# Query and key transposes by transposing DMA for the third and later blocks of a fused attention and channel-mix kernel

One core of a Trainium2 chip. The metric is the device time of one execution in microseconds (us), lower is better. Times below are medians of several executions; "span" is the length of one profiled execution. A run is called slow here when it lies over 1.5% above the fastest of the same kernel in the same call, and fast otherwise. The granted clock is the share of its full speed that TensorE was given, as the profile records it.

## The reference

Retention attention (a state that decays by gamma at each token), followed by an RWKV channel mix. Cut to what matters; the kernel computes the recurrence in chunks of 128 tokens.

```python
# q, k, v: (4, 8, 768, 64) float32
for t in range(S):
    state = gamma * state + k[:, :, t] (outer) v[:, :, t]
    y[:, :, t] = q[:, :, t] @ state / sqrt(D)
x = y.transpose(0, 2, 1, 3).reshape(B, S, 512)
xk = mu_k * x + (1 - mu_k) * x_prev          # x_prev: x one token earlier
xr = mu_r * x + (1 - mu_r) * x_prev
kk = max(xk @ w_k, 0)                         # 512 -> 1024
out = sigmoid(xr @ w_r) * (kk * kk @ w_v)
```

There are 24 chunks of 128 tokens, two to a block, so 12 blocks (0 to 11).

## The kernel before

The order of all instructions is written by hand: `at(t, fn, ...)` puts a piece of work at a place `t`, all pieces are sorted by `t` and emitted, and each engine runs its own in that order. Twelve units are one block in the steady stage. Semaphores that make a reader wait for its writer follow from the tiles. `keys` and `squared` below are the channel mix's first product and its relu and square; "gate" is the product with `w_r`, "values" the one with `w_v`.

```python
ORDER = {"att": {"scale": (-11.82,), "first": (-6.14, 0.23),
                 "T": (-2.09, 2.5), "TC": (-0.47, 4.83),        # transposes, their copy
                 "S": (2.27, 4.47), "A": (3.18, 6.35), ...,     # state, scores
                 "dx": (11.71,), "xk": (18.04, 21.12), "xr": (21.16, 27.83)},
         "mix": {"G": (-1.27, -0.4, 3.31, 4.49), ...},
         "load": (1.19, 3.99),
         "start": {0: (-6.29, -4.12, -3.14, -2.71), ...}}       # places of blocks 0 to 3
# ... cut ...
def scale_k(n, c, eng):                  # POOL for blocks 2 to 11, DVE for 0 and 1
    ...
    eng.tensor_tensor(out=KS[n][:, e], in0=K32[n][:, e], in1=w, op=ALU.mult)

def transposes(c):                       # 16 on TensorE for one chunk
    PT[c] = psa.tile([P, 2, NJ, C], F16, name="pT", tag="a")
    needs(("ks", c))
    for i, src in enumerate((Q16, KS)):
        for h in range(H):
            r = slice(h % 2 * D, h % 2 * D + D)
            nc.tensor.transpose(PT[c][r, i, h // 2, :], heads(src, c, h, 1), ident)

def transposed(c):                       # ACT copies them from PSUM to SBUF
    QKT[c] = att.tile([P, 2, NJ, C], F16, name="qkT")
    nc.scalar.copy(out=QKT[c], in_=PT.pop(c))

def scores(c):                           # pA = ks . q, from qkT alone
    ... nc.tensor.matmul(PA[c][hp][:, j, :], lhsT=QKT[c][r, 1, j, :], rhs=QKT[c][r, 0, j, :], ...)

def differ(m, eng):                      # dx = x - x_prev, POOL from block 2 on
    ... eng.tensor_tensor(out=DX[m], in0=xcur, in1=xprev, op=ALU.subtract)
# ... cut ...
def attention(n, t0, w=1.0):
    start = n < 2
    if not start:
        at(o("scale"), scale_k, n, None, nc.gpsimd)
    if n + LDK < NBLK:                   # the key load of block n+2 right behind the scaling of n
        at((... if start else o("scale")) + 0.01, load_k, n + LDK)
    for i, c in enumerate((2 * n, 2 * n + 1)):
        at(o("T", i), transposes, c)
        at(o("TC", i), transposed, c)
        # ... state, scores, mask, result ...
# ... cut: first loads, all at one place, so in the order of these lines ...
for n in range(2):
    for c in range(2):
        at(t, load_q, n, c); at(t, load_k, n, c); at(t, load_v, n, c)
at(t, load_wk, 0); at(t, load_wk, 1)
at(t, load_q, 2); at(t, load_v, 2)
at(t, load_wr); at(t, load_wv, 0); at(t, load_wv, 1)
```

## Time and profile before

| | kernel before |
|---|---|
| time, median of 3 runs | 174.53 us (173.55 to 176.16) |
| span of the profiled run | 173.3 us, mean granted TensorE clock 0.961 |
| TensorE (PE) busy / idle in the span | 152.7 / 20.6 us |
| PE idle in the first 80 us | 16.5 us |
| hardware DMA queue of SP (keys, stores) | 11.64 MB, 27.0% of 16 engines |

DVE is VectorE, ACT ScalarE, POOL GpSimd, SP SyncE. An L number is a line of that kernel's own file, so the same work has other L numbers in another kernel. The first 80 us of PE alone; columns: stretch, length, PE busy (instructions), granted clock, DMA share (packet time over that of 16 engines; it goes above 1 here), GB/s:

```profile
20.00:40.00 20.00, 16.82 (x282) 0.83 1.37 178
40.00:60.00 20.00, 16.51 (x216) 0.83 1.11 124
60.00:80.00 20.00, 20.00 (x344) 1.00 1.26 158
```

PE has a few us of holes between 20 and 60 us and none after. The second view is the chain of waits in that ramp (start, length, what):

```profile
22.89 1.91 POOL ks L185
24.80 12.01 issue
36.85 1.90 POOL dx L286
38.74 1.86 POOL ks L185
...
43.23 6.52 DMA v<-in_v_dram
```

POOL scales the keys of block 2 at 22.89 us, waits for the difference of block 2 (36.85), scales block 3's keys right behind it and only then issues block 3's last loads. In the ramp the blocks thus hang on each other through POOL. The start of a block's difference `dx` is a good milestone for its progress, and I use it below.

### The profile page before, as it was taken

Reading aid. Unit: us, or ns where it says so; the run is one execution under the profiler, and the core shown is the slowest. Engines: PE = TensorE matmul, PEld = TensorE weight load, DVE = VectorE, ACT = ScalarE, POOL = GpSimd, SP = SyncE. Lnnn points to the kernel's source line nnn. Section 1 sums busy time; section 2 is a strip of 40 time slices with the busy share of each in tenths; the row PEclk is TensorE's granted clock in tenths of the full one; section 3 lists DMA queues with packets and bytes.
Section 4 is the critical chain, followed back from the end, with each engine's and each line's share of the span. In section 5 each row is a group of like instructions: output and inputs, shape, how many; then the busy total and the mean of one; then the engine's idle time right before and its main releaser. Section 6 shows DMA issues by size and latency. Waiting matters only on the chain.

```text
span 173.3 us, 5544 instructions
## 1 busy us (share of the span) xinstructions
PE 152.7 (88%) x2448; PEld 112.7 (65%) x2448; DVE 133.5 (77%) x232; ACT 92.0 (53%) x146; POOL 88.0 (51%) x81
## 2 busy tenths in 40 slices
PE   0477759999659999999999999999999999999990
PEld 0345549776436865977958759669588587595940
DVE  3469999958655995879989979898799797795312
ACT  3132207957220592881954927729739459275750
POOL 7999260049903996097974926909726040040000
PEclk9999957999956999999999999999999999999999
DMA  6999999995998399919999499697993003030303
GB/s 51 196 177 224 202 165 175 193 192 58 158 212 94 94 202 201 214 29 153 158 144 162 114 199 116 90 190 153 67 58 123 1 11 118 0 118 7 125 0 123
DMA packets 78504, 21.96 MB, mean 127 GB/s; under 512 B 72464, under 2 KB 75152, under 8 KB 78480
## 3 DMA queue, kind: packets, MB, share of 16 engines
q0 software_dynamic: 52880, 9.97, 68.0%
q1 hardware_dynamic: 24544, 11.64, 27.0%
q8 instruction: 19, 0.31, 0.7%
q10 hardware_dynamic: 1056, 0.00, 0.3%
q14 instruction: 5, 0.04, 0.1%
HBM read 24.22 MB, written 6.29 MB: 176 GB/s over the span
## 4 chain that ended last, share of the span: by engine, by line
PE 69%; POOL 11%; DMA 9%; issue 8%; DVE 0%; POOLq 0%; DVEq 0%
PE pV L157 23%; PE pZ L157 21%; PE pR L157 10%; DMA wk<-in_moe_w_k_dram 6%; PE pT L197 4%; DMA v<-in_v_dram 4%; PE pA L208 3%; POOL q L169 3%; PE pY L261 3%; POOL v L169 2%; POOL ks L185 2%; POOL k L169 2%; PE pY L157 2%; PE pS L235 2%; POOL dx L286 1%
## 5 line engine op out<-in xcount | busy, mean ns | idle before, releaser
L286 POOL TENSOR_TENSOR dx<-xT 128x1024 f32<-128x1024 f32 x10 | 18.9, 1890 | 62.0 <-DVE xT L272 62.0
L157 PE MATMUL pZ<-xk,wk 128*64 128x256 f16 x768 | 48.4, 278 | 2.0 <-DVE xk L294 2.0
L157 PE MATMUL pV<-wv,k 128*64 128x512 f16 x384 | 48.3, 389 | 0.0
L157 PEld LDWEIGHTS <-wk 128*64 128x64 f16 x768 | 42.2, 112 | 4.4 <-issue 2.6
L201 ACT COPY qkT<-pT 128x1024 f16<-128x1024 f16 x24 | 24.1, 1004 | 38.2 <-PE pT L197 38.2
L315 ACT ACTIVATE kr<-pZ 128x512 f32<-128x512 f32 x48 | 28.3, 590 | 25.3 <-PE pZ L157 25.3
L216 DVE TENSOR_TENSOR a2t<-pA,c_sb 128x512 f16<-128x512 f32 x48 | 30.6, 683 | 11.2 <-PE pA L208 11.1
L157 PEld LDWEIGHTS <-k 128*64 128x64 f16 x384 | 21.1, 112 | 15.3 <-issue 1.4
L316 ACT ACTIVATE k<-kr 128x512 f16<-128x512 f32 x48 | 30.2, 630 | 1.5
L294 DVE SCALAR_TENSOR_TENSOR xr<-dx,mur,xT 128x256 f16<-128x256 f32 x48 | 29.7, 662 | 0.0
L294 DVE SCALAR_TENSOR_TENSOR xk<-dx,muk,xT 128x256 f16<-128x256 f32 x48 | 26.4, 597 | 2.0 <-POOL dx L286 2.0
L346 DVE SCALAR_TENSOR_TENSOR osb<-pV,rsb 128x512 f32<-128x512 f32 x24 | 15.9, 686 | 11.5 <-ACT rsb L329 8.4
L157 PE MATMUL pR<-wr,xr 128*64 128x512 f16 x192 | 23.1, 379 | 0.0
L169 POOL DMA_DIRECT2D q<-in_q_dram x24 | 22.1, 930 | 0.8 <-POOLq L488 0.8
L169 POOL DMA_DIRECT2D v<-in_v_dram x24 | 21.6, 919 | 0.0
L185 POOL TENSOR_TENSOR ks<-k,csm_sb 128x1024 f16<-128x1024 f32 x10 | 19.5, 1946 | 0.1
L272 DVE TENSOR_TENSOR xT<-pY,gy_sb 128x512 f32<-128x512 f32 x24 | 16.3, 687 | 2.6 <-PE pY L261 2.2
L329 ACT ACTIVATE rsb<-pR 128x512 f32<-128x512 f32 x24 | 13.0, 594 | 8.9 <-PE pR L157 8.9
L157 PEld LDWEIGHTS <-xr 128*64 128x64 f16 x192 | 11.0, 110 | 8.7
L244 DVE TENSOR_TENSOR sbd<-pS,csm_sb 128x512 f16<-128x512 f32 x20 | 13.7, 686 | 3.4 <-PE pS L235 2.6
L197 PE MATMUL pT<-c_sb,q 128*64 128x128 f16 x192 | 10.3, 232 | 5.5 <-DMA q<-in_q_dram 5.5
L197 PE MATMUL pT<-c_sb,ks 128*64 128x128 f16 x192 | 10.3, 231 | 2.8 <-DVE ks L185 2.8
(29 smaller groups left out, 105.5 us busy)
## 6 DMA issues: line engine op xcount, KB each, us to landing
out_dram<-osb SPq DMA_DIRECT2D x24, 256.0 KB, 4.0
k<-in_k_dram SPq DMA_DIRECT2D x20, 256.0 KB, 6.7
q<-in_q_dram POOLq DMA_DIRECT2D x24, 128.0 KB, 6.0
v<-in_v_dram POOLq DMA_DIRECT2D x24, 128.0 KB, 7.0
k<-in_k_dram POOLq DMA_DIRECT2D x4, 256.0 KB, 4.7
wk<-in_moe_w_k_dram POOLq DMA_DIRECT2D x2, 512.0 KB, 11.0
wv<-in_moe_w_v_dram POOLq DMA_DIRECT2D x2, 512.0 KB, 20.7
wr<-in_moe_w_r_dram POOLq DMA_DIRECT2D x1, 512.0 KB, 18.5
```

The source lines that it names most:

```text
L157: nc.tensor.matmul(out[r], lhsT=lhsT[:, r], rhs=rhs, skip_group_check=True, **kw)
L169: eng.dma_start(out=tiles[n][:, i], in_=rows(x, n)[:, i])
L185: eng.tensor_tensor(out=KS[n][:, e], in0=K32[n][:, e], in1=w, op=ALU.mult)
L197: nc.tensor.transpose(PT[c][r, i, h // 2, :], heads(src, c, h, 1), ident)
L201: nc.scalar.copy(out=QKT[c], in_=PT.pop(c))
L216: nc.vector.tensor_tensor(out=A2[c][:, hp], in0=PA[c][hp], in1=causal[:, None, :].to_broadcast([P, NJ, C]), op=ALU.mult,)
L272: nc.vector.tensor_tensor(out=xT[b][:, :, col : col + C], in0=PY.pop(c), in1=gy[:, c % 2], op=ALU.mult)
L286: eng.tensor_tensor(out=DX[m], in0=xcur, in1=xprev, op=ALU.subtract)
L294: nc.vector.scalar_tensor_tensor(out=dst[m][:, j], in0=DX[m][:, j], scalar=mu[:, j : j + 1], in1=xprev[:, j], op0=ALU.mult, op1=ALU.add,)
L315: nc.scalar.activation(out=kr, in_=PZ.pop((m, g)), func=AF.Relu)
L316: nc.scalar.activation(out=K2[m][:, 2 * g : 2 * g + 2], in_=kr, func=AF.Square)
L346: nc.vector.scalar_tensor_tensor(out=osb, in0=PV.pop((m, tb)), scalar=1.0 / (KSC * KSC), in1=RS.pop((m, tb)), op0=ALU.mult, op1=ALU.mult,)
```

## The change

Its intent: let a transposing DMA from SBUF to SBUF, issued by SP, do the transposes of chunks 4 to 23. PE loses sixteen instructions a chunk and ACT a copy. I call such a DMA a **crossing**. Queries and scaled keys go to one joint tile so that one DMA takes both. The whole hand-written order was tuned anew for this, and the first loads were interleaved anew. Core of the diff:

```diff
-        "scale": (-11.82,),
+        "scale": (-11.05,),
-        "T": (-2.09, 2.5),
-        "TC": (-0.47, 4.83),
+        "T": (-4.56, -0.31),
+        "TC": (-3.48, 6.58),
-        "A": (3.18, 6.35),
+        "A": (3.91, 7.67),
+        "k": (-23.59, -24.74),
+        "X": (-10.19, -4.73),
 ... cut: the other places of att, mix, load; those of start: ...
-        1: (-5.55, -2.96, -2.96, 0.0),
-        2: (-3.52, 0.96, 0.84, 1.45),
+        1: (-5.65, -3.49, -3.0, -0.14),
+        2: (-3.62, 1.74, 1.31, 1.67),
+    "first": {
+        "q": (-1.51, 5.3, 5.61, 9.72, 14.97, 23.84),
+        "k": (-1.12, 4.35, -0.45, 7.83),
+        "v": (-18.35, 8.91, 9.2, 11.06, 12.33, 21.01),
+        "wk": (10.81, 12.84),
+        "wr": (19.87,),
+        "wv": (19.65, 40.81),
+    },
+    "k": (-68.52, -56.85, -36.23, -32.51),
 ... cut ...
+    def crossed(c):
+        needs(("ks", c), ("q", c))
+        QKT[c] = qkp.tile([P, 2, NJ, C], F16, name="qkT")
+        nc.sync.dma_start_transpose(
+            out=QKT[c].rearrange("p i j t -> p (i j) t"),
+            in_=QK[c // 2][:, c % 2].rearrange("p i h d -> p (i h d)"),
+        )
 ... cut ...
-        if n + LDK < NBLK:
-            at((max(o("first", 0), o("first", 1)) if start else o("scale")) + 0.01, load_k, n + LDK)
+        if n > 3:
+            for i in range(2):
+                at(o("k", i), load_k, 2 * n + i, nc.sync)
-            at(o("T", i), transposes, c)
-            at(o("TC", i), transposed, c)
+            if start:
+                at(o("T", i), transposes, c)
+                at(o("TC", i), transposed, c)
+            else:
+                at(o("X", i), crossed, c)
 ... cut ...
+    for c in range(4, 8):
+        at(ORDER["k"][c - 4], load_k, c, nc.scalar)
```

More of the change, by code (lines that the diff above doesn't have):

```diff
@@ L17 @@
     "att": {
-        "scale": (-11.82,),
-        "first": (-6.14, 0.23),
-        "T": (-2.09, 2.5),
-        "TC": (-0.47, 4.83),
-        "S": (2.27, 4.47),
-        "SE": (3.82, 11.21),
-        "A": (3.18, 6.35),
-        "M": (5.96, 7.66),
-        "Y": (8.04, 9.34),
-        "YE": (8.05, 9.72),
-        "dx": (11.71,),
-        "xk": (18.04, 21.12),
-        "xr": (21.16, 27.83),
+        "scale": (-11.05,),
+        "first": (-9.81, -5.48),
+        "T": (-4.56, -0.31),
+        "TC": (-3.48, 6.58),
+        "S": (2.2, 7.51),
+        "SE": (3.63, 8.08),
+        "A": (3.91, 7.67),
+        "M": (6.21, 8.81),
+        "Y": (8.52, 9.14),
+        "YE": (10.96, 11.66),
+        "dx": (12.09,),
+        "xk": (17.49, 19.63),
+        "xr": (21.75, 27.19),
+        "k": (-23.59, -24.74),
+        "X": (-10.19, -4.73),
     },
     "mix": {
-        "G": (-1.27, -0.4, 3.31, 4.49),
-        "K": (0.71, 3.37, 5.32, 9.07),
-        "R": (5.49, 5.1),
-        "RS": (9.95, 9.96),
-        "V": (7.7, 9.1, 4.91, 9.14),
-        "O": (12.13, 13.29),
-    },
-    "load": (1.19, 3.99),
-    "pw": (-105.55, -78.0),
+        "G": (-1.7, 0.91, 2.49, 3.52),
+        "K": (2.46, 2.52, 4.44, 7.83),
+        "R": (5.55, 8.88),
+        "RS": (12.88, 12.9),
+        "V": (7.05, 12.83, 4.47, 10.23),
+        "O": (14.45, 14.22),
+    },
+    "load": (1.83, 2.36),
+    "pw": (-109.18, -78.05),
     "start": {
-        0: (-6.29, -4.12, -3.14, -2.71),
-        1: (-5.55, -2.96, -2.96, 0.0),
-        2: (-3.52, 0.96, 0.84, 1.45),
-        3: (-0.17, 2.67, 1.83, 3.0),
-    },
+        0: (-6.24, -3.73, -3.34, -2.98),
+        1: (-5.65, -3.49, -3.0, -0.14),
+        2: (-3.62, 1.74, 1.31, 1.67),
+        3: (0.33, 3.14, 2.29, 3.16),
+    },
+    "first": {
[7 more added lines that the diff above has]
+    "k": (-68.52, -56.85, -36.23, -32.51),
 }
@@ L106 @@
     att = pool("att", 4)
+    qkp = pool("qkp", 6)
     mid = pool("mid", 2)
@@ L133 @@
     ctx.enter_context(tc.manual_schedule())
-    K32, Q16, V16, KS, PT, QKT, PA, A2 = {}, {}, {}, {}, {}, {}, {}, {}
+    K32, QK, V16, PT, QKT, PA, A2 = {}, {}, {}, {}, {}, {}, {}
     PSS, SBD, PY, DX, XK, XR, K2, RS, PV = {}, {}, {}, {}, {}, {}, {}, {}, {}
@@ L157, in halves, with tokens, load_k, load_q @@
             nc.tensor.matmul(out[r], lhsT=lhsT[:, r], rhs=rhs, skip_group_check=True, **kw)
-    def rows(x, n):
-        b, t0 = 2 * n // NCH, 2 * n % NCH * C
-        return x[b, :, t0 : t0 + TM, :].rearrange("h (c t) d -> t c h d", t=C)
-    def load(n, c, x, eng, tiles, name, dt):
-        if n not in tiles:
-            tiles[n] = (ldk if dt is F32 else ld).tile([P, 2, H, D], dt, name=name)
-        for i in range(2) if c is None else (c,):
-            eng.dma_start(out=tiles[n][:, i], in_=rows(x, n)[:, i])
-    def load_k(n, c=None):
-        load(n, c, k, nc.sync if c is None else nc.gpsimd, K32, "k32", F32)
-    def load_q(n, c=None):
-        load(n, c, q, nc.gpsimd, Q16, "q16", F16)
-    def load_v(n, c=None):
-        load(n, c, v, nc.gpsimd, V16, "v16", F16)
+    def tokens(x, c):
+        b, ci = divmod(c, NCH)
+        return x[b, :, ci * C : ci * C + C, :].rearrange("h t d -> t h d")
+    def load_k(c, eng):
+        n, i = divmod(c, 2)
+        if n not in K32:
+            K32[n] = ldk.tile([P, 2, H, D], F32, name="k32")
+        eng.dma_start(out=K32[n][:, i], in_=tokens(k, c))
+    def load_q(c):
+        n, i = divmod(c, 2)
+        if n not in QK:
+            QK[n] = ld.tile([P, 2, 2, H, D], F16, name="qk16")
+        nc.gpsimd.dma_start(out=QK[n][:, i, 0], in_=tokens(q, c))
+        done.add(("q", c))
+    def load_v(c):
+        n, i = divmod(c, 2)
+        if n not in V16:
+            V16[n] = ld.tile([P, 2, H, D], F16, name="v16")
+        nc.gpsimd.dma_start(out=V16[n][:, i], in_=tokens(v, c))
     def scale_k(n, c, eng):
-        if n not in KS:
-            KS[n] = att.tile([P, 2, H, D], F16, name="ks16")
+        if n not in QK:
+            QK[n] = ld.tile([P, 2, 2, H, D], F16, name="qk16")
         e = slice(0, 2) if c is None else slice(c, c + 1)
         w = gk[:, e, :, None].to_broadcast([P, e.stop - e.start, H, D])
-        eng.tensor_tensor(out=KS[n][:, e], in0=K32[n][:, e], in1=w, op=ALU.mult)
+        eng.tensor_tensor(out=QK[n][:, e, 1], in0=K32[n][:, e], in1=w, op=ALU.mult)
         done.update(("ks", 2 * n + i) for i in range(e.start, e.stop))
-    def heads(tiles, c, a, n):
-        return tiles[c // 2][:, c % 2, a : a + n, :]
+    def ks(c, h):
+        return QK[c // 2][:, c % 2, 1, h]
+    def vs(c, h, n=1):
+        return V16[c // 2][:, c % 2, h : h + n, :]
     def transposes(c):
@@ L193, in transposes @@
         needs(("ks", c))
-        for i, src in enumerate((Q16, KS)):
+        needs(("q", c))
+        for i in range(2):
             for h in range(H):
                 r = slice(h % 2 * D, h % 2 * D + D)
-                nc.tensor.transpose(PT[c][r, i, h // 2, :], heads(src, c, h, 1), ident)
+                nc.tensor.transpose(PT[c][r, i, h // 2, :], QK[c // 2][:, c % 2, i, h], ident)
+    def crossed(c):
[5 more added lines that the diff above has]
+        )
     def transposed(c):
-        QKT[c] = att.tile([P, 2, NJ, C], F16, name="qkT")
+        QKT[c] = qkp.tile([P, 2, NJ, C], F16, name="qkT")
         nc.scalar.copy(out=QKT[c], in_=PT.pop(c))
@@ L236, in state @@
                     PSS[c][hp * D : hp * D + D, j, :],
-                    lhsT=heads(KS, c, 2 * j + hp, 1), rhs=heads(V16, c, 2 * j, 2),
+                    lhsT=ks(c, 2 * j + hp), rhs=vs(c, 2 * j, 2),
                     start=(first and j == 0), stop=(j == NJ - 1), skip_group_check=True,
@@ L261, in result @@
                 nc.tensor.matmul(
-                    PY[c][hp * D : hp * D + D, j, :], lhsT=heads(V16, c, 2 * j + hp, 1),
+                    PY[c][hp * D : hp * D + D, j, :], lhsT=vs(c, 2 * j + hp),
                     rhs=A2[c][:, hp, j, :],
@@ L354 @@
     T = 12.0
-    LDK = 2
     EV = ORDER["att"]
@@ L363, in attention @@
             at(o("scale"), scale_k, n, None, nc.gpsimd)
-        if n + LDK < NBLK:
-            at((max(o("first", 0), o("first", 1)) if start else o("scale")) + 0.01, load_k, n + LDK)
+        if n > 3:
+            for i in range(2):
+                at(o("k", i), load_k, 2 * n + i, nc.sync)
         for i, c in enumerate((2 * n, 2 * n + 1)):
@@ L445 @@
     t = -9.0 * T
-    at(t, constants)
-    for n in range(2):
-        for c in range(2):
-            at(t, load_q, n, c)
-            at(t, load_k, n, c)
-            at(t, load_v, n, c)
-    at(t, load_wk, 0)
-    at(t, load_wk, 1)
-    at(t, load_q, 2)
-    at(t, load_v, 2)
-    at(t, load_wr)
-    at(t, load_wv, 0)
-    at(t, load_wv, 1)
+    L0 = ORDER["first"]
+    at(t - 20.0, constants)
+    for c in range(6):
+        at(t + L0["q"][c], load_q, c)
+        at(t + L0["v"][c], load_v, c)
+        if c < 4:
+            at(t + L0["k"][c], load_k, c, nc.gpsimd)
+    for c in range(4, 8):
+        at(ORDER["k"][c - 4], load_k, c, nc.scalar)
+    for h in range(2):
+        at(t + L0["wk"][h], load_wk, h)
+        at(t + L0["wv"][h], load_wv, h)
+    at(t + L0["wr"][0], load_wr)
     LQ = ORDER["load"]
-    for n in range(3, NBLK):
-        at((n - 4) * T + LQ[0], load_q, n)
-        at((n - 4) * T + LQ[1], load_v, n)
+    for c in range(6, NC):
+        o = (c // 2 - 4) * T + 2.0 * (c % 2)
+        at(o + LQ[0], load_q, c)
+        at(o + LQ[1], load_v, c)
     at(ORDER["pw"][0], powers)
```

## The prediction

> **What bounds the kernel now.** I read the page first (busy times, the row of 40 slices, the chain that ended last), then the table of stretches with one stretch for each block period, then the instructions in order of time, the list of waits and the DMA issues. The page says TensorE (PE) and points at no other engine:
>
> ```profile
> span 173.3 us, 5544 instructions
> PE 152.7 (88%) x2448; PEld 112.7 (65%) x2448; DVE 133.5 (77%) x232; ACT 92.0 (53%) x146; POOL 88.0 (51%) x81
> ...
> PE   0477759999659999999999999999999999999990
> ...
> DVE  3469999958655995879989979898799797795312
> ...
> PEclk9999957999956999999999999999999999999999
> ```
>
> PE is full from about 50 us to the end and has holes only before. An average of 88% hides two stages: a **ramp** of some 50 us, in which the first loads, the first attention blocks and VectorE (DVE) set the pace, and a **steady stage** in which PE never rests. Cutting the steady stage at the same point of successive blocks (the start of the first gate product's chain piece) gives the period, and what the other engines do in it. Columns: stretch, its length, busy time of PE, weight loads, DVE, ACT, POOL, granted clock, DMA share, GB/s:
>
> ```profile
> 87.24:99.04 11.80, 11.80 (x204) 8.73 (x202) 11.00 (x20) 7.69 (x13) 8.15 (x8) 1.00 1.06 140
> 99.04:110.84 11.80, 11.80 (x204) 8.73 (x202) 10.37 (x19) 7.28 (x12) 7.05 (x7) 1.00 1.05 134
> 110.84:122.64 11.80, 11.80 (x210) 8.84 (x208) 10.21 (x18) 7.49 (x13) 7.28 (x7) 1.00 1.09 154
> 122.64:134.44 11.80, 11.80 (x205) 8.73 (x202) 10.74 (x19) 7.70 (x13) 5.78 (x5) 1.00 0.84 91
> 146.24:156.26 10.02, 10.02 (x155) 7.24 (x152) 7.78 (x16) 5.28 (x10) 1.89 (x1) 1.00 0.14 51
> 156.26:164.93 8.67, 8.67 (x114) 6.21 (x112) 3.65 (x8) 5.65 (x11) 0.00 (x0) 1.00 0.18 65
> ```
>
> One block of 256 tokens takes 11.80 us, PE 11.80 of it. DVE is second with a mean of 10.58 us in the first four rows; ACT and POOL have over 3 us to spare. The last two rows are blocks with no attention left beside them: the change cannot shorten those. A busy PE might still be one that waits inside, so I read the chain of waits in order of time, which shows PE pieces back to back (start, length, what):
>
> ```profile
> 101.09 0.98 PE pV L157 x8
> 102.52 1.73 PE pV L157 x16
> 104.70 0.45 PE pT L197 x16
> 105.14 1.75 PE pZ L157 x32
> 107.33 0.45 PE pT L197 x16
> 107.78 0.33 PE pA L208 x8
> 108.11 1.87 PE pZ L157 x32
> ```
>
> The transposes are on this path, 0.45 us for the sixteen of one chunk of 128 tokens. The small holes between the pieces are products left out of the short list.
>
> **What the Trainium skill says.** (1) "TensorE: Matmul & The Clock Gate", section "Part 4: PE-mode transpose", gives about 275 ns for one transpose in a kernel's context. The trace has a median of 219 ns for one, but they overlap: sixteen in 0.45 us are 28 ns each, so the duration of one must not be multiplied by the count (it would give 3.5 us a chunk, eight times too much). Even the group's busy time, 1.23 us a period, counts the pipeline's tail; the chain's 0.45 us is what I use. (2) "Advanced Engine Details and Errata", section "X-Bar Transpose (TRN2)", holds that transposing DMAs are as fast as regular ones; (3) "DMA: Bandwidth & Descriptors", section "Latency and other measured facts", gives 261 GB/s for one with a non-contiguous middle dimension. No run of the kernel before has such a DMA, so the trace can't agree or disagree. (4) "SBUF — State Buffer", section "SBUF: two separate sides", says that GpSimd and some DVE operations lock each other out of a shared port pair. The trace agrees in kind: the mixing operation on DVE has a median of 476 ns and a maximum of 2565 ns, and the long ones lie beside POOL's 1.9 us operations. The change leaves both of those where they are.
>
> **The change, part by part.** *Removed*, for chunks 4 to 23 (20 of 24): sixteen PE transposes with their weight loads, one PSUM slot for the result (there are four in that pool, and a chunk takes 1 for the transposes beside 2 for scores, 1 for results and half of one for the state), and one ACT copy. The profile's rows:
>
> ```profile
> L201 ACT COPY qkT<-pT 128x1024 f16<-128x1024 f16 x24 | 24.1, 1004 | 38.2 <-PE pT L197 38.2
> L197 PE MATMUL pT<-c_sb,q 128*64 128x128 f16 x192 | 10.3, 232 | 5.5 <-DMA q<-in_q_dram 5.5
> L197 PE MATMUL pT<-c_sb,ks 128*64 128x128 f16 x192 | 10.3, 231 | 2.8 <-DVE ks L185 2.8
> ```
>
> ACT loses 20 x 1.0 = 20 us, all beside other work, so it is worth nothing directly. On PE, chunks 4 to 7 are transposed in the ramp (29.8 to 45 us), where PE has idle time anyway: nothing there. Chunks 8 to 23 are sixteen pieces of 0.45 us in the chain from 62.5 to 142.7 us: 16 x 0.45 = **7.2 us** on the path. That is the ceiling for the steady stage. The period would go from 11.80 to 10.90 us.
>
> But DVE's work in a period is 10.58 us and does not shrink. DVE would be busy 10.58 of 10.90, 97%, where it is 90% now, on an in-order engine that waits for scores, results and POOL's differences. That can't be filled without some stalls; I choose 0.2 us of each period's 0.9 as lost, so of 7.2 us some 5.6 us remain (7.2 x 0.7 / 0.9).
>
> *Added*: 20 transposing DMAs of 128 x 1024 f16, 256 KB each, issued by SP. For the time to landing the nearest rows are:
>
> ```profile
> out_dram<-osb SPq DMA_DIRECT2D x24, 256.0 KB, 4.0
> k<-in_k_dram SPq DMA_DIRECT2D x20, 256.0 KB, 6.7
> q<-in_q_dram POOLq DMA_DIRECT2D x24, 128.0 KB, 6.0
> ```
>
> At the skill's 261 GB/s the bytes alone take 1.0 us, an estimate; with the 4.0 us of a store as the lower end and the 6.7 us of a key load as the upper, I take 4 to 7 us from issue to landing. In the new order the DMA stands 14.1 (first chunk) and 12.4 units (second) ahead of the scores that need it; twelve units are a period of 10.9 us, so there are 12.8 and 11.3 us. The POOL scaling, 1.9 us, stands just ahead of it and takes some 1.5 us from the first. The latency is hidden with about 4 us to spare. SP spends most of its time waiting for results to store (101 us in the list of waits), and its key-load issues take 0.37 to 1.6 us: two more a period fit if they cost that. Traffic: two DMAs add 0.5 MB to the 1.6 MB of a period (134 GB/s x 11.8 us), and loads end by 128 us, well ahead of their use, so the slowing of loads by a third is absorbed.
>
> *Moved*: the first loads are interleaved in another order, key loads of chunks 4 to 7 go to ACT's queue in place of SP's, the value weights come later, and in steady operation the q and v loads alternate by chunk ahead of the scaling. The ramp has a PE stall of some 3 us before 49.8 us, where the state product waits for the values of block 3, whose load was issued only after POOL's difference and scaling; it is followed by a stretch at 0.74 of the clock (50 to 60 us). The new order puts those loads ahead of that scaling (1.9 us earlier), but then the scaling comes 3.6 us later and the DMA's 4 to 7 us come after it, where PE took 1 us. In the ramp the DMA path is longer, not shorter. I put the ramp at 1 us of gain, from the 1.9 us, with 3 us either way.
>
> **Sum**: 174.5 - 5.6 - 1 = 167.9 us, rounded to 168.
>
> **The rivals.** *First: the DMAs themselves are slow.* If one needs 12 us or more, or SP is held for over 5 us issuing one, then scores wait for the crossing, stores stand behind it on SP, and the steady period grows: two 6 us issues a period exceed 10.9 us, and fourteen periods' worth of that ends at 180 us or above. For it: nothing of the kind is in the trace, and DMA queues are already at a share of 1.05. Against: the skill's two figures, and the order leaves 11 us. One chance in seven. *Second: DVE becomes the bound with most of the gain lost.* DVE's 10.58 us becomes the period plus 0.6 us of waiting, 11.2 to 11.4: some 3.5 us gained, 171 us. For it: 11.00 us busy in one period. Against: part of DVE's time is lock time, which moves. One in five. *Third: the ramp decides.* The whole second load of blocks 2 and 3 now passes through one more DMA latency while queues are fullest; if PE starts its full stage 3 to 4 us later, 4 us of the gain go, and the result is 171 to 172 us. Or the stall before 50 us and the slow clock after it vanish, worth up to 5 us: 163 us.
>
> **Range and chances.** The ceiling without the ramp is 174.5 - 7.2 = 167.3; with the ramp's best, 162.5. Low end 162.5. High end 176, where the DMAs wait now and then. Faster by over 2% is below 171.0: my centre is 3 us inside it, and the first rival and half of the other two lie outside: 0.66. Within 2%: 0.18. Slower (above 178) is almost only the first rival: 0.16.
>
> **What would show it right or wrong.** Right: full periods of 10.9 to 11.2 us with PE still full in the table of stretches; no wait of scores for the crossed tile in the list of waits; crossing DMAs landing in 4 to 7 us; ACT near 72 us busy; DVE at 95% or more of the period. Wrong step "latency hidden": PE waits for the crossed tile by DMA, or SP's own waits grow and stores come late. Wrong step "0.45 us a chunk": periods shorten by clearly more or less than 0.9 us with PE full. Wrong step "ramp 1 us": the first full PE slice comes earlier or later than 50 us by more than 3 us. The prediction is wrong as a whole if a transposing DMA costs much more than a plain one of its size.

## The result

| | before | after |
|---|---|---|
| time, median (lowest to highest), 4 runs each, same rounds | 175.31 us (173.55 to 176.16) | 184.45 us (183.46 to 184.93) |
| span of the profiled run, mean clock | 173.3 us, 0.961 | 183.1 us, 0.944 |
| PE busy / idle | 152.7 / 20.6 us | 145.5 / 37.6 us |
| PE idle in the first 80 us | 16.5 us | 31.5 us |
| ACT busy | 92.0 us | 76.0 us |

The change made the kernel 5% slower: ratio 1.0528, 95% interval 1.0425 to 1.0631. A ratio here and below is the mean time of one kernel's fast runs over that of the other's of the same rounds, so it is not quite the ratio of the medians quoted. Both profiles are of fast runs.

From the page after, the first lines that answer to those of before (span, PE in 40 slices of 4.6 us):

```profile
span 183.1 us, 4944 instructions
...
PE   0266553959920759999899999999989999999991
```

PE's busy time falls by 7.2 us (152.7 to 145.5) and its idle time grows by 17.0 us, 15.0 of it in the first 80 us. That the 7.2 is the predicted figure is luck: the prediction counted 16 chunks, while PE lost the transposes of 20 (320 instructions, some 9.0 us at 0.45), and other products took longer (pZ 48.4 to 50.9 us, pV 48.3 to 50.8, pR 23.1 to 25.2). The full stage begins with slice 15 (69 us, slices counted from 0), in the kernel before with slice 12 of slices of 4.33 us (52 us). The stretches of PE, columns as above:

```profile
20.00:40.00 20.00, 12.46 (x178) 0.83 1.36 165
40.00:60.00 20.00, 11.44 (x148) 0.87 1.06 115
60.00:80.00 20.00, 17.24 (x216) 0.79 1.40 180
```

The chain of waits in the ramp after shows what PE waits for:

```profile
17.59 9.54 DMA k<-in_k_dram
...
27.30 2.01 POOL qk L200
...
29.32 9.42 DMA qkT<-qk
...
38.78 0.40 PE pA L236 x8
...
44.07 1.90 POOL dx L314
...
59.06 7.32 DMA k<-in_k_dram
```

Block 2's scaling starts at 27.30 us (22.89 before) because its key load was issued on ACT's queue at 17.59 and landed at 27.13. The crossing then takes 9.42 us, and the difference of block 2 starts at 44.07 (36.85 before). Block 4's keys hold POOL up again at 59 to 66 us. Block 3 is not in this chain, but PE's instructions show its scores wait longest, 8.95 us:

```profile
60.88 0.61 PE L236 MATMUL pA<-qkT 64*128 64x128 f16 x8 [8.95 <-DMA qkT<-qk]
```

The clock may be a part of the loss too: from 60 to 80 us it was 0.79, in the kernel before 1.00. No run here separates that from the waits.

From the DMA issues, the crossing beside the key load of the same size and queue (count, KB, median us from issue to landing; the crossing's row has no size):

```profile
k<-in_k_dram SPq DMA_DIRECT2D x16, 256.0 KB, 7.2
...
qkT<-qk SPq DMA_TRANSPOSE x20, 7.3
```

Its minimum, median and maximum:

```profile
DMA to landing us min/median/max: 3.1/7.3/9.9
```

The steady stage, cut at successive starts of `dx` (columns as in the prediction's table of stretches, all engines):

```profile
105.41:116.94 11.53, 11.34 (x182) 8.32 (x178) 11.04 (x19) 6.00 (x10) 7.45 (x7) 1.00 1.72 179
116.94:127.86 10.92, 10.92 (x174) 7.93 (x170) 10.43 (x18) 5.99 (x10) 7.45 (x6) 1.00 1.43 200
127.86:139.39 11.53, 11.07 (x172) 8.13 (x168) 11.04 (x19) 5.88 (x10) 7.46 (x7) 1.00 1.80 143
```

Here the change does what it was meant to. The mean period from block 6 to block 11 is 11.26 us against 11.84 before, cut the same way. DVE is busy 32.51 of these 33.98 us, 96%. After 75 us PE waits only 0.2 us in all for a crossed tile; before 75 us it waits 11.1 us, in two waits (8.9 us for block 3, 2.2 us for block 2).

The milestones as a ledger (start of `dx` of block n, us):

| kernel | dx2 | dx3 | dx5 | dx11 | span |
|---|---|---|---|---|---|
| before | 36.85 | 54.91 | 82.41 | 152.79 | 173.3 |
| after | 44.07 | 71.06 | 94.33 | 161.69 | 183.1 |
| difference | +7.2 | +16.2 | +11.9 | +8.9 | +9.8 |

Everything is lost by block 3. Between blocks 3 and 5 some 4 us come back, between 5 and 11 another 3.0 us, and the tail loses 0.9, which I did not follow up.

### The profile page after: what moved, and what is told of

Same layout as the page of the kernel before. It is cut to its first block, busy times and chain, and to the rows that moved or that the text cites. A ratio compares the mean times of both kernels' runs of the same rounds, so it can differ in the third digit from the quotient of the medians.

```text
span 183.1 us, 4944 instructions
## 1 busy us (share of the span) xinstructions
PE 145.5 (79%) x2128; PEld 104.9 (57%) x2128; DVE 135.1 (74%) x232; ACT 76.0 (41%) x126; POOL 88.8 (48%) x81
## 3 DMA queue, kind: packets, MB, share of 16 engines
q1 hardware_dynamic: 41504, 15.83, 47.5%
## 4 chain that ended last, share of the span: by engine, by line
PE 36%; DVE 26%; DMA 20%; POOL 11%; issue 2%; ACT 1%; SPq 0%; POOLq 0%
PE pV L169 13%; PE pZ L169 12%; DMA k<-in_k_dram 9%; DVE a2t L244 8%; DVE xk L322 6%; DMA qkT<-qk 5%; DVE xr L322 5%; PE pR L169 4%; DMA v<-in_v_dram 3%; POOL dx L314 3%; DVE sbd L272 3%; DMA qk<-in_q_dram 3%; POOL qk L186 2%; POOL qk L200 2%; DVE osb L374 2%
## 5 line engine op out<-in xcount | busy, mean ns | idle before, releaser
L169 PE MATMUL pZ<-xk,wk 128*64 128x256 f16 x768 | 50.9, 281 | 4.6 <-DVE xk L322 4.5
L169 PE MATMUL pV<-wv,k 128*64 128x512 f16 x384 | 50.8, 390 | 0.0
L169 PEld LDWEIGHTS <-wk 128*64 128x64 f16 x768 | 44.3, 114 | 8.8 <-issue 5.7
L322 DVE SCALAR_TENSOR_TENSOR xr<-dx,mur,xT 128x256 f16<-128x256 f32 x48 | 33.1, 729 | 0.0
L169 PEld LDWEIGHTS <-k 128*64 128x64 f16 x384 | 21.8, 112 | 14.5 <-issue 1.7
L200 POOL TENSOR_TENSOR qk<-k,csm_sb 128x1024 f16<-128x1024 f32 x10 | 20.1, 2008 | 17.3 <-DMA k<-in_k_dram 17.3
L169 PE MATMUL pR<-wr,xr 128*64 128x512 f16 x192 | 25.2, 386 | 0.0
L186 POOL DMA_DIRECT2D qk<-in_q_dram x24 | 22.1, 924 | 1.7 <-DMA wk<-in_moe_w_k_dram 1.7
L236 PE MATMUL pA<-qkT 64*128 64x128 f16 x192 | 10.2, 229 | 12.2 <-DMA qkT<-qk 11.3
L169 PEld LDWEIGHTS <-xr 128*64 128x64 f16 x192 | 11.1, 113 | 8.0 <-issue 0.4
L300 DVE TENSOR_TENSOR xT<-pY,gy_sb 128x512 f32<-128x512 f32 x24 | 15.6, 678 | 0.1
L236 PEld LDWEIGHTS <-qkT 64*128 64x128 f16 x192 | 5.8, 98 | 17.0 <-DMA qkT<-qk 12.0
L289 PE MATMUL pY<-a2t,v 128*64 128x128 f16 x192 | 12.1, 231 | 4.2 <-DVE a2t L244 4.1
## 6 DMA issues: line engine op xcount, KB each, us to landing
wv<-in_moe_w_v_dram POOLq DMA_DIRECT2D x2, 512.0 KB, 16.2
```

The source lines that it names most:

```text
L169: nc.tensor.matmul(out[r], lhsT=lhsT[:, r], rhs=rhs, skip_group_check=True, **kw)
L186: nc.gpsimd.dma_start(out=QK[n][:, i, 0], in_=tokens(q, c))
L200: eng.tensor_tensor(out=QK[n][:, e, 1], in0=K32[n][:, e], in1=w, op=ALU.mult)
L322: nc.vector.scalar_tensor_tensor(out=dst[m][:, j], in0=DX[m][:, j], scalar=mu[:, j : j + 1], in1=xprev[:, j], op0=ALU.mult, op1=ALU.add,)
```

## The experiments

My theory after the result: the crossing's latency stands in the serial chain of the ramp, so transposing blocks 2 and 3 on PE, with all else as after, should bring the gain back. Rivals: the new order and loads of the ramp are late by themselves; or the crossings cost in the steady stage too.

### Which part costs the time

**e1_pe_ramp**: after, with PE transposes in blocks 2 and 3 as well.

```diff
+        "T2": (-2.09, 2.5),  "TC2": (-0.47, 4.83),     # the places of the kernel before
-            if start:
+            if n < 4:
```

> The changed kernel, with blocks 2 and 3 (chunks 4 to 7) transposed by TensorE and copied by ScalarE again; crossing DMAs only from block 4 on; first loads as in the changed kernel. Ramp-by-crossing theory (the ramp is late by 9 to 12 us because the crossings of chunks 4 to 7 put a DMA's 7 to 9 us where TensorE took 1 us, and because the key loads of block 4 stand behind them in SyncE's queue): the difference of block 2 starts by 40 us, that of block 3 by 58 us, and the time is 172 to 175 us. Ramp-by-load-order theory (the new order of the first loads is what makes it late): time stays at 180 us or more. Both: steady period stays 11.3 us, because VectorE sets it.

Measured: 181.24 us against 173.54, ratio 1.0494 (1.0367 to 1.0622). The expected return did not come: the ratio overlaps that of after. The milestones say the same more finely: dx3 67.89 (after 71.06), dx5 91.04 (94.33). The crossing theory's marks (dx3 by 58 us, 172 to 175 us) failed, and the rival's (180 us or more) came. Taking the crossings out of blocks 2 and 3 returns 3.3 us of 11.9. Two things show why not more. Block 2's scaling starts at 29.00 us, as late as in after, since its keys come as late (POOL waits 18.0 us for keys in all). And in PE's order, 5.33 us of mix products of block 1 (pZ) stand ahead of the scores of block 2 (pA), as the new order puts them; the clock in these 5.33 us was 0.68.

```profile
31.62 5.33 PE L171 MATMUL pZ<-xk,wk 128*64 128x256 f16 x64
...
38.64 0.40 PE L238 MATMUL pA<-qkT 64*128 64x128 f16 x8
```

In the kernel before, the scores of block 2 start at 31.65 us and 1.94 us of those products follow them. It looks as if the new order was built around a late crossed tile: with the tile early, the scores stay late.

**e2_no_cross**: after without any crossing; edit as e1 with `if n < 12:`.

> The changed kernel with all chunks transposed by TensorE and ScalarE: only the new order of loads and work is left of the change. Ramp-by-crossing theory: the ramp is as in the run with TensorE for blocks 2 and 3, the steady period is back to 11.8 us or a little above; time 174 to 179 us. Ramp-by-load-order theory: 184 us or more.

Measured: 190.84 us, ratio 1.1078 (1.0942 to 1.1213): a miss for the crossing theory; the rival's 184 us or more came, but partly by a longer steady period, which neither theory had. The ramp is as in e1 (dx3 67.97, dx5 90.83), and the period rises to 12.89. So the new order without its crossings is slower in the steady stage than the kernel before (11.84). The places of the transposes came from the kernel before and were not tuned here, so the size of it proves little; it does show that the order and the crossings belong together, and that the ramp's loss stays without any crossing.

**e3_cross_old_order**: the kernel before, its order and loads kept, with crossings from block 2 on.

```diff
+        "X": (-8.0, -4.73),
+    qkp = pool("qkp", 6)          # and the joint tile for q and ks
-            at(o("T", i), transposes, c)
-            at(o("TC", i), transposed, c)
+            if n < 2:
+                at(o("T", i), transposes, c)
+                at(o("TC", i), transposed, c)
+            else:
+                at(o("X", i), crossed, c)
```

> The kernel before, with its own order of first loads and of work, and crossing DMAs from block 2 on (placed in front of the scores by a similar lead). Ramp-by-crossing theory: late in the ramp by 6 us or more at the difference of block 3, time 178 us or more. Ramp-by-load-order theory: no later than the kernel before in the ramp, steady period 11.3 us, time 169 to 172 us.

Measured: 210.16 us, ratio 1.2015 (1.1797 to 1.2233); its profile fell in a slow run. With dx3 at 77.11 us, 22 us late, the crossing theory's mark came here. Crossings landed in 3.0/7.9/16.5 us (minimum, median, maximum) and PE waited 38.4 us for them. Where the crossings stand in the old order (the places in `X`) was not tuned. So placed, the old order has no room for them, whereas the new order has some: of the two, the new order is the one that limits the damage.

**e4_keys_ahead**: after, with the steady key loads nearly a block (some 10 of 12 units) earlier.

```diff
-        "k": (-23.59, -24.74),
+        "k": (-34.0, -33.9),
```

> The changed kernel with one thing moved: the key loads of blocks 4 and later are put in SyncE's queue right behind the first crossing two blocks earlier, so those of block 4 stand ahead of the crossings of block 3. If the waiting of key loads behind crossings (8 us of the ramp: keys of block 4 issued at 58.5 us and landed at 66.4 us) is a part of the loss by itself: the scaling of block 4 starts by 56 us and the time falls by 3 to 6 us, to 178 to 181 us. If the crossing's own latency is all: no change, 184 us.

Measured: 186.65 us, ratio 1.0796 (1.064 to 1.0952): no gain. The scaling of block 4 came at 63.0 us in place of 66.5, yet dx5 moved from 94.33 to 96.58. The keys came only 3.5 us sooner and not the 10 expected, and now the crossings came later (11.5 us at most, and PE waited 15.1 us for them). So taking a little off POOL's wait for block 4's keys did not bring the block forward, and the test is a weak one.

### Loads, work order, or both

The next call asked whether the key loads on ACT's queue, the first loads or the order of work make the ramp late.

**e5_keys_early**: after, with all key loads issued two blocks ahead by SP as in the kernel before, those on ACT's queue dropped.

```diff
-        if n > 3:
+        if n + 2 < NBLK:
+                tk = max(o("first", 0), o("first", 1)) if start else o("scale")
-                at(o("k", i), load_k, 2 * n + i, nc.sync)
+                at(tk + 0.01, load_k, 2 * (n + 2) + i, nc.sync)
-    for c in range(4, 8):
-        at(ORDER["k"][c - 4], load_k, c, nc.scalar)
```

> The changed kernel, but with the key loads where the kernel before has them: all from SyncE's queue, two blocks ahead, right behind the scaling that frees their buffer (so those of blocks 2 and 3 at about 10 us and those of block 4 at about 27 us, ahead of every crossing and every store). The last runs showed the ramp late also without crossings. New theory, keys: the lateness comes from the keys, of block 2 (landed at 27 us on ScalarE's queue) and of block 4 (issued at 58 us, behind stores and crossings). Then the scaling of block 2 starts by 24 us, the difference of block 3 by 62 us, and the time is 175 to 179 us. Rival, order: the program order of TensorE in the ramp (first gate products ahead of the scores of block 2) and of the other loads is the cause: within 2 us of 184.

Measured: 200.59 us against 173.96, ratio 1.163 (1.1533 to 1.1727). Now the crossings stand behind the key loads on SP's queue: they land in 3.0/7.6/14.5 us, and PE waits 24.7 us for them, the longest 15.6. Neither expectation held (175 to 179 us, or within 2 us of 184): the scaling of block 2 did come early, at 23.81 us, but with the keys of later blocks back on SP's queue the ramp is far worse.

**e6_pe_ramp_keys**: e1 and e5 together.

> The same key loads, and blocks 2 and 3 transposed by TensorE. Keys theory: the crossings of blocks 2 and 3 cost their 3 us again, so 171 to 176 us, difference of block 3 by 58 us. Order theory: 179 to 182 us, as without the key loads moved.

Measured: 188.33 us (185.16 to 188.66), no ratio given. The profile is of the fastest run (dx5 93.48, e1: 91.04). No gain over e1, and neither expectation (171 to 176 us, 179 to 182 us) held; three of the four runs are slow and they scatter by 3.5 us, so I read no more from it.

**e7_pe_ramp_old_loads**: e6 with the first loads in the order of before.

```diff
-    for c in range(6):
-        at(t + L0["q"][c], load_q, c)
 ... cut ...
+    for c in range(4):
+        at(t, load_q, c)
+        at(t, load_k, c, nc.gpsimd)
+        at(t, load_v, c)
+    at(t, load_wk, 0); at(t, load_wk, 1)     # then q, v of block 2, wr, wv, as before
```

> As the run before in this list, and GpSimd's first loads (queries, keys, values, weights) in the order of the kernel before too. If the order of those loads mattered beside the keys: 2 to 4 us less than the run before in this list. If not: within 1.5 us of it.

Measured: 183.51 us, ratio 1.051 (1.0385 to 1.0635); dx5 90.57. Old loads alone give back 0.5 us at dx5 against e1 (2.9 us against e6, whose key loads it shares).

**e8_hybrid**: e7 with the old order of work as well for blocks 0 to 3 and the old places of mix for blocks 0 and 1. All up to block 3 is now as before; crossings and the new order begin with block 4.

```diff
+    "att0": { ... the places of before ... },
+    "mix0": { ... the places of before ... },
+        ev = ORDER["att0"] if n < 4 else EV
+        MX = ORDER["mix0"] if m < 2 else ORDER["mix"]
```

> The whole ramp of the kernel before (its first loads, its places in time for blocks 0 to 3, TensorE transposes there) joined to the steady stage of the changed kernel (crossings from block 4 on). Both theories: the ramp as before, differences of block 3 by 57 us, then periods of 11.3 us against 11.84: 169 to 172 us, faster than both kernels. If the crossings also disturb what the ramp left to do, 173 to 176 us.

Measured: 180.78 us, ratio 1.0444 (1.0315 to 1.0573). dx3 is 53.38, so the ramp up to block 3 is repaired (before: 54.91), and dx5 is 86.60. PE waited 6.9 us for crossed tiles; chunk 8's was issued at 59.34 us and landed at 68.5. The expected 169 to 172 us, or 173 to 176, did not come: the loss had moved to the first blocks that cross.

**e9_pe_old_work**: the missing corner, e1 with the old work order for blocks 0 to 3 and the new loads.

> The changed kernel with TensorE transposes for blocks 2 and 3, its new first loads kept, and only the places in time of the work of blocks 0 to 3 (start table, attention offsets, mixing offsets of blocks 0 and 1) as in the kernel before. Work-order theory (the ramp is late because the retuned order puts the gate products of block 1 ahead of the scores of block 2 on TensorE, with the other engines to match): difference of block 2 by 40 us and of block 3 by 58 us, against 43.9 and 67.9 in the run with only the crossings of blocks 2 and 3 undone; time 173 to 177 us. First-load theory (those loads make it late whatever the work order): within 2 us of that run's 181.2.

Measured: 180.42 us against 171.42, ratio 1.048 (1.0395 to 1.0565); dx3 59.62, dx5 90.46. The time is the one expected if the first loads make the ramp late (within 2 us of e1), though dx3 comes near the other theory's 58 us. POOL waited 10.2 us for block 2's keys, whose scaling began at 31.94 us. The four corners, all with PE transposes in blocks 2 and 3:

| dx3 / dx5 | new work order | old work order |
|---|---|---|
| new loads | 67.89 / 91.04 (e1) | 59.62 / 90.46 (e9) |
| old loads | 64.25 / 90.57 (e7) | 53.38 / 86.60 (e8) |

At block 3 both parts count: new loads alone +6.2, new work order alone +10.9, both +14.5. At block 5 each alone costs about 4 us and both together 4.4. Either is enough to make the ramp late, so undoing one at a time shows almost nothing, and the table does not divide the loss between them. By the ratios alone the four can't be told apart (1.044 to 1.051); the table rests on one profile each.

### Where crossings begin, and the steady stage

**e10_hybrid6**: e8 with PE transposes up to block 5.

```diff
-            if n < 4:
+            if n < 6:
```

> Ramp, first loads and key loads of the kernel before, TensorE transposes for blocks 0 to 5, crossings from block 6 on with the changed kernel's steady order. In the hybrid with crossings from block 4 the lag came at blocks 4 and 5: the crossing of chunk 8 landed 9.2 us after issue, its scores had waited 3.8 us. If a crossing's latency is the cause there: difference of block 5 by 83.5 us (86.6 in that run), time 175 to 178 us. If the joint of the two orders is the cause: no gain, 180 us.

Measured: 177.36 us, ratio 1.0283 (1.0184 to 1.0382). dx5 83.90: the crossings of blocks 4 and 5 had cost 2.7 us. But the first that is left, of block 6, shows the same again in its chain:

```profile
79.06 10.75 DMA qkT<-qk
```

The scores waited 2.2 us for it, and block 6's period was 13.36 us. From block 6 to 11 the period is 11.26, exactly that of after, so this stage can be tested apart from the ramp:

**e11_h6_mask_early**: e10, with the first chunk's scores and mask placed earlier.

```diff
-        "A": (3.91, 7.67),   "M": (6.21, 8.81),
+        "A": (1.6, 7.67),    "M": (3.15, 8.81),
```

> As the run before in this list, with the first chunk's scores and masking moved 2 to 3 units earlier, so that masking, which has one operand in PSUM, stands on VectorE beside GpSimd's scaling, and not the mixing operations with two SBUF operands, which take 2.6 us a pair there in place of 0.8. If VectorE with its locked time sets the steady period (11.3 us): 0.3 to 0.8 us less a period over the seven last periods, 2 to 5 us less. If not: same within 1 us.

Measured: 176.67 us, ratio 1.0258 (1.0126 to 1.0391). DVE's busy time in the profile fell from 135.2 to 126.6 us, as the mean of the mixing operation xr fell from 698 to 520 ns (in e10 every second pair of it takes 2.67 us in place of 0.87, beside POOL's 2.0 us scaling), and the period stayed at 11.29. That does not show that shorter DVE operations are worth nothing. One of the five periods is 11.89 us long, with a 1.0 us wait of the scores for a crossed tile, and e10 has no such wait in this stretch: scores placed earlier leave the crossing less time. Without that 1.0 us the mean would be 11.1. The edit changed two things at once and does not separate them.

**e12_half_mask**: e10 with half the mask, a wrong result on purpose (relative error 0.676), to take 0.68 us of DVE work off each chunk.

```diff
-        for hp in range(2):
+        for hp in range(1):            # one half masked, read by both products
-                    rhs=A2[c][:, hp, j, :],
+                    rhs=A2[c][:, 0, j, :],
```

> Wrong on purpose: as the hybrid with crossings from block 6, but only one half of the heads is masked, which takes 2 x 0.6 us a period from VectorE and nothing from TensorE, ScalarE or the DMAs. If VectorE sets the steady period: 10.7 to 11.0 us a period, and TensorE full again, 3 to 5 us less in time. If the crossings' latency sets it: no change.

Measured: 171.41 us, ratio 0.9877 (0.9746 to 1.0009); its profile fell in a slow run, though with the clock at 1.00 in the steady stage. The period there is 10.97 us, near the 10.90 that the prediction gave PE alone, with PE full and DVE well below the period in stretches such as this:

```profile
107.72:118.36 10.64, 10.64 (x170) 7.46 (x166) 8.97 (x16) 5.99 (x10) 7.29 (x6) 1.00 1.87 183
```

So half of the masking costs 0.29 us of the steady period (11.26 to 10.97), at least as far as a slow run may be set beside a fast one; one of these five periods (11.78 us) holds a 0.5 us wait for a crossing as well. The edit also shortens the path from scores to result, so it does not show whether DVE's load or that path counted. The time fell by 6 us against e10, more than five such periods; where the rest came from stays open.

**e13_hybrid2**: the counterpart of e8: old loads and order in the ramp, but crossings from block 2 on.

```diff
+        "X": (-8.0, -4.73),            # in att0
-            if n < 4:
+            if n < 2:
```

> Ramp, first loads and key loads of the kernel before, but with crossings from block 2 on, and the steady order of the changed kernel from block 4 on: the earlier hybrid (crossings from block 4, 180.8 us, difference of block 3 at 53.4 us) with the crossings of blocks 2 and 3 added. Crossing-latency theory (in the ramp each block's attention hangs on the block before, so each crossing adds its 7 to 9 us to the chain, where TensorE takes 1 us): difference of block 2 at 45 to 47 us in place of 38.7, of block 3 at 66 to 70 us, time 188 us or more. If the crossings of the ramp cost only what undoing them in the changed kernel gave back (3 us): difference of block 3 by 58 us, time 184 us.

Measured: 204.12 us against 171.99, ratio 1.1939 (1.1837 to 1.2041). Against e8 the crossings of blocks 2 and 3 now cost 11.3 us at dx2 (49.98), 22.3 at dx3 (75.66) and 24.6 at dx5. In the chain of this kernel:

```profile
27.05 15.96 DMA qkT<-qk
43.05 0.61 PE pA L262 x8
```

In the new order the same crossings cost 3.3 us (after against e1). The new loads and order thus hide most of this latency, at a price of their own. (The place -8.0 was not tuned, and the clock from 0 to 90 us was 0.83 in this run against 0.89 in after: both are in the 24.6.)

**e14_old_cross8** and **e15_old_cross10**: the kernel before in everything, with crossings only for blocks 8 to 11, or 10 and 11. Edit as e3, with `"X": (-10.5, -9.0)` and `if n < 8:` or `if n < 10:`.

> The kernel before, its loads and order, with crossings only for blocks 8 to 11, issued right behind the scaling. The removed 8 x 0.45 us of TensorE are 3.6 us; if the crossing's latency is covered by the 9 us between scaling and scores, 171 to 173 us beside 174; if it is not, scores wait and the time is 176 us or more.

Measured: 174.72 us, ratio 1.019 (1.0058 to 1.0322): slower by the interval, unclear at the 2% that the verdicts use, and between the two expectations. Its chain has this piece, which PE's scores of block 8 waited for:

```profile
97.39 10.91 DMA qkT<-q
```

dx8 is 3.4 us later than before (120.77 against 117.39), although dx7 had been 1.9 us earlier: the period that ends at dx8 took 17.09 us in place of 11.80. PE waited 3.4 us in it, and its granted clock was 0.80 where the periods beside it have 1.00. Removing eight chunks' transposes (3.6 us by the prediction's 0.45) did not outweigh that. The periods after it are worth a look (columns as in the steady stage above):

```profile
120.77:131.46 10.69, 10.69 (x172) 7.72 (x170) 10.39 (x18) 5.77 (x10) 7.49 (x7) 1.00 0.97 121
131.46:142.58 11.12, 11.12 (x182) 8.05 (x180) 10.72 (x19) 5.77 (x10) 3.75 (x2) 1.00 0.78 125
```

In the kernel before the same two took 11.58 and 12.02 us, and the next 11.80 against 10.91 here. So once no crossing is waited for, each block is shorter by 0.89 to 0.90 us, the whole of the predicted 0.9, with PE full and DVE busy 97% and 96% of the period. The last three periods of e3, also in the old order, are the same within 0.01 us (10.68, 11.13 and 10.90).

> As the run before in this list, for blocks 10 and 11 only, where the loads have ended and the DMA queues are quiet (a crossing landed in 3.1 us there). 4 x 0.45 us are 1.8 us: 172 to 173 us beside 174, no wait for a crossing; that would beat both kernels by 1%, inside the noise of one run but not of the fast means.

Measured: 171.69 us (168.91 to 174.81, 9 runs) against 171.99 (11 runs), ratio 0.9875 (0.9803 to 0.9948), within 2%. By the fast runs that is 1.2% faster than before and the fastest correct version tried; but only four of its nine runs are fast, and over all runs the medians differ by 0.3 us. Its crossings (two issued from 120.8 us, beside the last loads of queries and values, and two from 132.4 us, after them):

```profile
DMA to landing us min/median/max: 3.0/4.8/7.7
```

The first two landed in 7.2 us in the median, the last two in 3.1, and PE waited for none. Its profile is labelled slow; against that of before, dx11 is 2.2 us earlier and the span 2.2 us shorter, and PE is full from the ramp to the end. Of the 2.2 us, 0.4 were there at dx9, before any crossing. The two blocks that cross gave 1.79 us (dx9 to dx11 22.03 us against 23.82), and four chunks of 0.45 us are 1.8 us.

## Why the prediction was wrong

Predicted were 168.0 us and 162.5 to 176; 184.45 came. Step by step:

- **"What it removes" was right.** It is the periods of e14 and e15 that show it: 0.89 to 0.90 us a block, so 0.45 a chunk. PE's busy time in after also fell by 7.2 us, but by luck, as said above. (A small misreading: the transposes of chunks 4 to 7 run to 47.5 us in the kernel before, not to 45; and 167.3 less the ramp's best of 5 is 162.3, not 162.5.)
- **The steady stage went the right way, with a smaller size.** Of 0.9 us a period 0.58 remained (11.84 to 11.26); I had kept 0.7. The predicted mark of 10.9 to 11.2 us was just missed. The reason given, that DVE can't be filled to 97% without stalls, is not borne out: in the old order (e14) DVE is busy 96 to 97% of the period, PE stays full and the whole 0.9 us is kept. In after the 19 DVE operations of a period take 11.04 us, against 10.72 in e14's, and PE falls short of the period by up to 0.46 us. So the 0.3 us were lost in the new order and not by crossing as such. That its longer DVE operations did it fits e11 and e12 but is not shown by them alone. From block 5 to block 11 the change gains 3.0 us, and the tail takes back 0.9. The 5.6 us were counted over eight periods; two of those lie in what was really the ramp.
- **"4 to 7 us from issue to landing" was too low at the top.** The median is 7.3 us and the maximum 9.9 after; the maximum is 14.5 to 16.5 in the runs that cross blocks 2 and 3 with the key loads two blocks ahead on the same queue (e3, e5, e13). The median is not slower than a key load's 7.2, and with hardly a load beside them crossings landed in 3.1 to 3.2 us: they land late where the queues are full. Issues on SP stayed below the 5 us of my first rival in after (at most 4.07) and landings below its 12 us, so that rival does not hold in after. It does in e3 and e13 (issues of up to 10.1 and 10.6 us).
- **"The latency is hidden with about 4 us to spare" failed in the ramp**, and it is the main error together with the next. It holds after 75 us (0.2 us of waits). It was worked out from places in the order, 14.1 and 12.4 units, turned to time at the steady rate. In the ramp a place is no lead time: the crossing can only be issued when the scaling is done, the scaling waits for a key load and for POOL, and the scores are the next thing that PE could do. There the whole latency is on the path, 9.42 us from 29.32 to 38.74 for block 2, and block 3's scores wait 8.95 us.
- **"The ramp at 1 us of gain, with 3 either way" failed most.** It came to a loss of 11.9 us at dx5. I had seen both its terms, loads 1.9 us earlier and a DMA latency where PE took 1 us, and had let them cancel within a block. What failed is that they act in series through POOL's differences: 7.2 us late at block 2 became 16.2 at block 3.

The 11.9 us divide, by undoing parts in one order, into 3.3 for the crossings of blocks 2 and 3 (after to e1), 4.4 for loads and work order together (e1 to e8), 2.7 for the crossings of blocks 4 and 5 (e8 to e10) and 1.5 that is left (e10 against before). At dx11 the same steps are 3.3, 2.2, 2.7 and 0.8. Each step compares one profile with another, and the scatter is not small: before, e14 and e15 do the same work in the same order up to block 5 (apart from the joint tile) and have dx5 at 82.41, 80.50 and 82.04. So the 1.5 is inside the scatter, and the 2.7 and 3.3 not far outside it. In another order of undoing the numbers would differ greatly, as e13 shows: without the new loads and order the crossings cost 24.6 us. What is shown is that these two belong together. The new loads and order soften the crossings' latency and are late by themselves; with the crossings gone they have only their price. That the tuning put the mix products ahead of the scores because of the latency is an inference from e1's order, not shown.

My **third rival**, that the ramp decides, was right in kind: blocks 2 and 3 pass through one more DMA latency while the queues are fullest. I gave it 171 to 172 us, because I counted 3 to 4 us once and not once for each block of the chain. My theory after the result (crossings of blocks 2 and 3 alone) fell with e1.

Left open: how loads and work order share their 4.4 us, how much of the 3 us between after and e1 is run to run scatter (the kernel before alone ranged from 170.5 to 176.9 us over all calls; that step rests on the profiles), how much of the ramp's loss is the lower clock in the stretches with waits, and the tail's 0.9 us.

## What to carry to other kernels

When work moves from an engine to a DMA, count its latency separately in the ramp: once for each block of a serial chain, from the moment its input is ready, with the landing times of full queues, and not by its place in an order that was tuned for the steady stage. A replacement can be right for a few late blocks only; here four chunks out of twenty, beside and after the last loads, gave 1.8 us (1.2% by the fast runs), and crossing earlier ones as well cost more than it saved. An engine that is busy 96% of a period need not be what stalls another: look for the same share in an order that runs without stalls. If a change and a retuned order come together, undoing one part at a time can return almost nothing; test the corners.

## What the Trainium skill lacked or had wrong

- "Advanced Engine Details and Errata", section "X-Bar Transpose (TRN2)", holds transposing DMAs to be as fast as regular ones and names no load under which that holds. In time to landing under load this case agrees: 7.3 us against 7.2 for a key load of 256 KB on the same queue. In a quiet stretch (140 to 160 us of after) it does not quite: 3.2 us for two crossings against 2.2 for four stores of the same size (in e15, from 128 to 145 us, 3.1 against 2.1), though stores of the kernel before took 3.1 in its own stretch from 140 to 160 us. Issuing one also holds SP longer: 1.24 us at least, 1.65 in the median and 4.07 at most in after, up to 10.55 in e13, where a store's issue took 0.36 us and two key loads' 1.00 us in the kernel before.
- "DMA: Bandwidth & Descriptors", section "Latency and other measured facts", gives 261 GB/s. Here SP's queue went from 27.0% of 173.3 us to 47.5% of 183.1, 40.2 us more, although four key loads had moved to ACT's queue (3.7% of 183.1 less 0.3% of 173.3, 6.3 us). The sum of 46.5 us over 20 crossings is 2.3 us of all 16 engines for each, so some 114 GB/s. This is an estimate from those shares, taken beside other traffic, so it does not contradict the page. Near the end of after, from 148 to 149 us, where a crossing was the only transfer listed as still under way, the DMA engines moved 212 GB/s.
- No page that I found says how long a crossing waits behind DMAs already queued. The runs show landings of 9.4 us in after's ramp, 16.0 in e13, and in e15 7.2 in the median beside the last loads and 3.1 once they were over.
